# The second pass's x in the first pass's last stage: multiplication and low parts on GpSimd in place of VectorE

## The chip, the cores and the metric

One core of a Trainium2 chip runs the whole kernel. The metric is the device time of one execution in microseconds (us). TensorE (PE) does the matmuls, VectorE (DVE) and ScalarE (ACT) the work on elements, SyncE (SP) issues the DMAs, and GpSimd (POOL) has little to do. Each engine works through its own queue in order, and semaphores tie the queues together.

## The reference

An attention with capped scores, then two dense blocks with 768 inputs and 2048 inner columns:

```python
scores = cap * np.tanh((q @ k.T / sqrt(64)) / cap)       # 4 batches, 12 heads, 448 rows, 64 wide
attn = exp(scores - max) / (sum + 1e-09)
x = (attn @ v)  ->  (1792, 768)
h = x @ w_in;  x = (h - np.tanh(h)) @ w_out               # block 1
h = x @ w_in2; out = (h / (1 + np.exp(-1.702 * h))) @ w_out2   # block 2
```

All of it is float32 and the two weight matrices of a block come in float64.

## The kernel before

The 1792 rows are worked in two passes of two batches each (`NB = 2`, 896 rows per pass). The attention of all four batches comes first. Of batches 0 and 1 (first pass) its outputs stay on the chip; those of batches 2 and 3 (second pass) go to DRAM as 12 tiles `xd`, 128x448 each, together with rows `wrow` of reciprocal softmax sums. A pass then runs `gemm_in` and the output product of block 1, then block 2, whose last stage, `gemm_rows_seven`, writes the result.

Every matmul operand is split in two fp32r parts, a high part (a rounded copy: `hi_act` on ACT, line 76) and a low part (value minus high part: `lo_dve` on DVE, line 88, or `lo_pool` on GpSimd, line 82). A product is three matmuls: high x high, high x low, low x high. In the traces `wh`/`wl` are the parts of weights, `rh`/`rl` those of the left operand of the last stage, `xh`/`xl` those of x. As line 88 is one helper for all low parts, its rows are told apart by tile.

`gemm_rows_seven` (lines 967 to 1057) forms its product from seven smaller ones, p = 0 to 6, named in `SEVEN_B`. Each has four chunks of weights. `ahead` (line 1001) prepares the weights two chunks ahead (`LEAD = 2`, three buffers `wh`/`wl`): a DMA into `whole` or `pair`, the cast wh on ACT, the subtraction wl on DVE. `left(SEVEN_B[p + 1], k)` makes the left operand of the *next* small product (rh on ACT, rl on DVE). The results of a small product leave PSUM through line 985, 988 (`pair<-ps_o`, one PSUM and one SBUF input) or `rows_out` (lines 1063, 1069), which stores to DRAM. From p = 2 on, the first pass also does one step per chunk for the second pass's x: line 1027 loads a tile of x and its row sums (`x_load`: x in one of two buffers `far`, w in one of two buffers `t`, three DMAs on SP), and line 1025 scales the tile that was loaded two steps earlier (`x_scale`): x times w, the high part into `xh`, the low part into `xl`. A buffer of x is free for the next load once its low part is made. There are 12 tiles; all 12 pairs `xh`, `xl` are read in the first microseconds of the second pass (`gemm_in`, line 787).

In the attention stage GpSimd multiplies nothing; it casts and subtracts: the low parts of the first pass's x (`xl<-xs`, 128x448) and of nine early weight chunks (`wl<-wr`, 128x768).

Only the instructions of the attention stage are pinned to the order of the program (`pin`). In the later stages a scheduler at build time, by its own model of durations, sets the order in each engine's queue; on the chip that order is fixed.

Of the kernel before, what the change touches and what calls it, by code (L numbers as in the profile page):

```python
# [15 lines left out]
ALU = mybir.AluOpType  # L16
# [21 lines left out]
def attention_moe_moe(ctx, tc, q, k, v, cap, w_in1, w_out1, w_in2, w_out2, out):  # L38
    nc = tc.nc
    B, H, S, D = q.shape  # L40
# [31 lines left out]
    def pin(ins):  # L72
        return tc.keep_in_program_order(ins) if pinned[0] else ins

    def hi_act(dst, src):
        pin(nc.scalar.copy(out=dst, in_=src))  # L76
# [4 lines left out]
    def lo_pool(dst, src, hi):  # L81
        pin(nc.gpsimd.tensor_tensor(out=dst, in0=src, in1=hi.bitcast(F32), op=ALU.subtract))
# [4 lines left out]
    def lo_dve(dst, src, hi):  # L87
        pin(nc.vector.tensor_tensor(out=dst, in0=src, in1=hi.bitcast(F32), op=ALU.subtract))  # L88
# [12 lines left out]
    xh = [big.tile([P, NT], F32R, name=f"xh{i}") for i in range(KM)]  # L101
    xl = [big.tile([P, NT], F32R, name=f"xl{i}") for i in range(KM)]
# [432 lines left out]
    def x_split(s, i, x):  # L535
        a = slice(s * S, (s + 1) * S)
        hi_act(xh[i][:, a], x)
        lo_dve(xl[i][:, a], x, xh[i][:, a])
# [428 lines left out]
    def gemm_rows_seven(b0):  # L967
# [29 lines left out]
        for p, name in enumerate(SEVEN_B):  # L997
            ps = three()
            for j in range(KQ):
                i, (wh, wl) = w_next()  # L1000
                ahead(i)
                for kk in range(2):
                    k = 2 * j + kk
                    h, l = ring[k]
                    for n in range(3):
                        t = slice(n * P, (n + 1) * P)
                        for m, (x, w) in enumerate(((h, wh), (h, wl), (l, wh))):
                            nc.tensor.matmul(  # L1008
                                ps[n], x[:, t], w[:, kk, :],
                                start=(k == 0 and m == 0), stop=(k == KH - 1 and m == 2),  # L1010
                            )
                    if name == "11":
                        rest_products(k, k, 0, wh[:, kk, :], wl[:, kk, :], True, False)
                    elif name == "21":
                        rest_products(k, KH + k, 0, wh[:, kk, :], wl[:, kk, :], False, True)
                    elif name == "22":
                        rest_products(k, KH + k, 1, wh[:, kk, :], wl[:, kk, :], True, False)
                    if p < 6:
                        left(SEVEN_B[p + 1], k)
                if p == 0 and j == 0:  # L1020
                    run_late()
                if p < 2:
                    continue
                if len(loaded) > 1 or loaded and not todo:
                    x_scale(*loaded.pop(0))
                if todo:
                    loaded.append((*todo[0], *x_load(b0 + NB, *todo.pop(0))))
# [57 lines left out]
        return x, w  # L1085

    def x_scale(s, i, x, w):
        nc.vector.tensor_tensor(out=x, in0=x, in1=w, op=ALU.mult)
        x_split(s, i, x)

    def moe(b0):
        if b0 + NB == B:
# [76 lines left out]
```

## Time and profile before

| | |
|---|---|
| median of 3 runs | 1096.5 us (1094.42 to 1097.2) |
| profiled execution | 1100.42 us, of which the span of the trace is 1098.6 us |
| PE / DVE / ACT / POOL busy | 98% / 85% / 61% / 5% of the span |
| granted TensorE clock | 0.998 of full speed |

A row of the timeline gives start (us), duration (us), engine, line and operation, out<-in, and in brackets how long the engine idled before it and what ended that (`[1.17 <-DVE wl L88]`: 1.17 us, until the wl of line 88 on DVE was done). Consecutive instructions of an engine overlap in the records: the start of the next one tells when the engine was free, and an end is later than that. Matmuls are pipelined, so it is the distance between their starts that counts. Spans on POOL are rough.

### The profile page before, as it was taken

The numbers are of one execution on the slowest core, as the hardware profiler recorded it, in microseconds if no ns is written. First come the engines' busy times: TensorE is split into PE (matmuls) and PEld (weight loads), VectorE is DVE, ScalarE is ACT, GpSimd is POOL, SyncE is SP. The second block draws the span as 40 slices with busy tenths as digits, with TensorE's granted clock in tenths as the row PEclk, the third lists the DMA queues.
The fourth block names the chain that finished last, engine by engine and source line by source line (L and its number), as shares of the span: only waits on it lengthen the run. The fifth ranks groups of instructions, "written<-read, shape, count | busy, mean of one in ns | idle before, by whom it ended". The sixth has DMA issues, their size and how long they took to land.

```text
span 1098.6 us, 16113 instructions
## 1 busy us (share of the span) xinstructions
PE 1082.0 (98%) x5579; PEld 886.7 (81%) x5579; DVE 931.2 (85%) x1467; ACT 668.7 (61%) x1022; POOL 59.1 (5%) x56
## 2 busy tenths in 40 slices
PE   9999998999999999999999999999999999999998
PEld 3333333688899889889999998889999989999998
DVE  4788999799997787888796885899999898889774
ACT  6898888799893434444255554767655554455453
POOL 0013443200000000000000000000000000000000
PEclk9999999999999999999999999999999999999999
DMA  6766685455538899898735778888555243333344
GB/s 147 203 190 195 189 244 186 153 205 170 178 116 283 312 314 337 286 306 287 261 94 171 220 224 279 303 270 306 176 195 176 87 132 113 101 115 101 122 142 141
DMA packets 156466, 220.58 MB, mean 201 GB/s; under 512 B 58672, under 2 KB 108640, under 8 KB 156384
## 3 DMA queue, kind: packets, MB, share of 16 engines
q1 hardware_dynamic: 155088, 218.94, 62.4%
q8 instruction: 44, 0.72, 0.3%
q10 hardware_dynamic: 1296, 0.61, 0.2%
q14 instruction: 38, 0.31, 0.1%
HBM read 160.83 MB, written 58.68 MB: 200 GB/s over the span
## 4 chain that ended last, share of the span: by engine, by line
PE 71%; DVE 11%; DMA 7%; ACT 6%; issue 4%; SPq 1%; DVEq 0%; ACTq 0%
PE ps_h L787 21%; PE ps_o L1008 12%; PE ps_y L850 10%; PE ps_h L934 9%; PE ps_pv L497 7%; PE ps_sc L456 5%; DMA wd<-in_moe_w_out_dram 4%; PE ps_o L993 3%; DVE wr L185 1%; DVE wd L175 1%; DVE g_q L696 1%; DVE wl L88 1%; DVE g_t L694 1%; ACT wr L168 1%; PE ps_qk L435 1%
## 5 line engine op out<-in xcount | busy, mean ns | idle before, releaser
L787 PE MATMUL ps_h<-xl,wh 128*128 128x384 f32 (+1 forms) x576 | 210.6, 366 | 1.2 <-DVE xl L88 1.2
L787 PE MATMUL ps_h<-xh,wh 128*128 128x384 f32 (+1 forms) x576 | 209.5, 364 | 0.7 <-DMA wh<-kept 0.7
L76 ACT CAST rh<-gr 128x384 fp32r<-128x384 f32 (+1 forms) x141 | 73.8, 528 | 95.9 <-PE ps_o L1008 47.7
L787 PE MATMUL ps_h<-xh,wl 128*128 128x384 f32 (+1 forms) x576 | 131.1, 362 | 0.0
L787 PEld LDWEIGHTS ps_h<-xl,wh 128*128 128x128 f32 x576 | 108.1, 188 | 14.3 <-DVE xl L88 2.1
L787 PEld LDWEIGHTS ps_h<-xh,wh 128*128 128x128 f32 x576 | 108.1, 188 | 13.9 <-DMA wh<-kept 1.1
L1008 PE MATMUL ps_o<-wl,rh 128*128 128x384 f32 x336 | 112.6, 335 | 3.1 <-DVE wl L88 3.1
L76 ACT CAST wh<-whole 128x768 fp32r<-128x768 f32 (+1 forms) x105 | 84.8, 809 | 50.1 <-PE ps_h L934 37.1
L787 PEld LDWEIGHTS ps_h<-xh,wl 128*128 128x128 f32 x576 | 104.6, 188 | 12.6 <-issue 1.4
L1008 PE MATMUL ps_o<-wh,rh 128*128 128x384 f32 x336 | 112.3, 334 | 0.0
L1008 PE MATMUL ps_o<-wh,rl 128*128 128x384 f32 x336 | 112.2, 334 | 0.0
L88 DVE TENSOR_TENSOR wl<-whole,wh 128x768 fp32r<-128x768 f32 (+1 forms) x105 | 96.6, 923 | 7.9 <-ACT wh L76 6.7
L168 ACT ACTIVATE wr<-wd 128x768 f32<-128x768 f32 x64 | 57.9, 906 | 74.0 <-DMA wd<-in_moe_w_out_dram 37.8
L88 DVE TENSOR_TENSOR rl<-gr,rh 128x384 fp32r<-128x384 f32 (+1 forms) x141 | 79.9, 575 | 15.1 <-ACT rh L76 14.2
L475 ACT ACTIVATE t<-ps_sc,tsc 128x896 f32<-128x896 f32 x72 | 69.9, 1006 | 26.7 <-PE ps_sc L456 26.7
L175 DVE TENSOR_SCALAR wd<-wd 128x768 uint16<-128x768 uint16 x57 | 59.7, 1047 | 24.5 <-ACT wr L168 24.3
L477 ACT ACTIVATE t<-t,cpos 128x896 f32<-128x896 f32 x72 | 72.3, 1042 | 0.4
L812 PE MATMUL ps_y<-gh,wh 128*128 128x512 f32 (+1 forms) x192 | 70.0, 365 | 1.2 <-DVE xl L88 1.2
L812 PE MATMUL ps_y<-gl,wh 128*128 128x512 f32 (+1 forms) x192 | 69.9, 364 | 0.0
L456 PE MATMUL ps_sc<-qk 64*128 64x448 f32 x288 | 68.1, 571 | 0.8 <-ACT qk L76 0.6
L497 PE MATMUL ps_pv<-t,rv 128*64 128x448 f32 x288 | 64.4, 552 | 3.9 <-ACT t L475 3.4
L1008 PEld LDWEIGHTS ps_o<-wl,rh 128*128 128x128 f32 x336 | 63.1, 188 | 4.1 <-DVE wl L88 4.1
(145 smaller groups left out, 2311.3 us busy)
## 6 DMA issues: line engine op xcount, KB each, us to landing
wd<-in_moe_w_in_dram SPq DMA_DIRECT2D x64, 384.0 KB
wd<-in_moe_w_out_dram SPq DMA_DIRECT2D x32, 768.0 KB
single<-wr SPq DMA_DIRECT2D x48, 384.0 KB
whole<-single SPq DMA_DIRECT2D x43, 384.0 KB
pair<-single SPq DMA_DIRECT2D x40, 384.0 KB
s<-pair SPq DMA_DIRECT2D x32, 384.0 KB
whole<-s SPq DMA_DIRECT2D x32, 384.0 KB
wh<-kept SPq DMA_DIRECT2D x25, 384.0 KB
```

The costliest lines, as they stand in the source:

```text
L76: pin(nc.scalar.copy(out=dst, in_=src))
L88: pin(nc.vector.tensor_tensor(out=dst, in0=src, in1=hi.bitcast(F32), op=ALU.subtract))
L175: pin(nc.vector.tensor_scalar(out=half[:, :, 2], in0=half[:, :, 1], scalar1=F64_LOW, scalar2=None, op0=ALU.mult))
L456: pin(nc.tensor.matmul(ps[:, j, :S], qk[a, kc], qk[a, :S], start=True, stop=True))
L475: pin(nc.scalar.activation(out=t, in_=ps[:, :, :S], func=AF.Tanh, scale=tsc))
L477: ins = pin(nc.scalar.activation(out=tt[g, c], in_=tt[g, c], func=AF.Exp, scale=cpos))
L497: pin(nc.tensor.matmul(ps[a, :S], w, t[:, j], start=(c == 0), stop=(c == KC - 1)))
L787: pin(nc.tensor.matmul(ps, w[:, kk, :], x[kk][:, a], start=(m == 0), stop=(m == len(seq) - 1)))
L812: nc.tensor.matmul(bank[e][:, :a1 - a0], w[:, kk, c], x[2 * j + kk][:, a0:a1], start=(j == 0 and m == 0), stop=(j == KF // 2 - 1 and m == ...
L850: nc.tensor.matmul(ps[e], w[:, kk, c], x, start=(k == 0 and m == 0), stop=(k == KH - 1 and m == 2))
L934: nc.tensor.matmul(ps, w, x, start=(m == 0), stop=(m == len(seq) - 1))
L1008: nc.tensor.matmul(ps[n], x[:, t], w[:, kk, :], start=(k == 0 and m == 0), stop=(k == KH - 1 and m == 2),)
```

## The change

In `x_scale` the multiplication goes from DVE to GpSimd, the high part stays on ACT, and the low part goes from DVE (through `x_split`) to GpSimd. `x_scale` runs in the last stage of the first pass alone, 12 times.

```diff
     def x_scale(s, i, x, w):
-        nc.vector.tensor_tensor(out=x, in0=x, in1=w, op=ALU.mult)
-        x_split(s, i, x)
+        a = slice(s * S, (s + 1) * S)
+        nc.gpsimd.tensor_tensor(out=x, in0=x, in1=w, op=ALU.mult)
+        hi_act(xh[i][:, a], x)
+        lo_pool(xl[i][:, a], x, xh[i][:, a])
```

`x_split` was `hi_act` and `lo_dve` on the same tiles; `lo_pool` is the helper of line 82.

## Rows read from the trace of the kernel before

**Rows 1.** The page, busy us (share of the span) xinstructions: TensorE.
```profile
PE 1082.0 (98%) x5579; PEld 886.7 (81%) x5579; DVE 931.2 (85%) x1467; ACT 668.7 (61%) x1022; POOL 59.1 (5%) x56
```

**Rows 2.** Table of stretches: from:to us, length, then busy us (xinstructions) by engine.
```profile
core 0: us, PE busy (x) PEld busy (x) DVE busy (x) ACT busy (x) POOL busy (x), PEclk, DMA share, GB/s
598.00:650.00 52.00, 48.89 (x279) 47.93 (x278) 46.65 (x81) 32.21 (x56) 0.00 (x0) 1.00 0.71 217
650.00:664.00 14.00, 14.00 (x83) 14.00 (x82) 6.99 (x13) 3.28 (x5) 0.00 (x0) 1.00 0.68 205
```

**Rows 3.** Timeline of PE: the four waits between 598 and 666 us.
```profile
621.88 0.45 PE L1008 MATMUL ps_o<-wl,rh 128*128 128x384 f32 x1 [0.75 <-DVE wl L88]
...
626.48 0.44 PE L1008 MATMUL ps_o<-wl,rh 128*128 128x384 f32 x1 [1.19 <-DVE wl L88]
...
639.77 0.33 PE L1008 MATMUL ps_o<-wh,rl 128*128 128x384 f32 x1
639.94 0.34 PE L1008 MATMUL ps_o<-wh,rh 128*128 128x384 f32 x1
641.45 0.45 PE L1008 MATMUL ps_o<-wl,rh 128*128 128x384 f32 x1 [1.17 <-DVE wl L88]
...
665.18 0.50 PE L787 MATMUL ps_h<-xh,wh 128*128 128x512 f32 x1 [0.75 <-DMA wh<-kept]
```

**Rows 4.** Groups by line and shape, DVE, 598 to 650 us: busy us, mean ns | idle.
```profile
L88 DVE TENSOR_TENSOR rl<-gr,rh 128x384 fp32r<-128x384 f32 x23 | 12.3, 551 | 0.1
L88 DVE TENSOR_TENSOR wl<-whole,wh 128x768 fp32r<-128x768 f32 x11 | 10.4, 951 | 0.0
L1088 DVE TENSOR_TENSOR x<-x,w 128x448 f32<-128x448 f32 x12 | 7.4, 620 | 4.6 <-DMA x<-xd 2.8 <-DMA w<-wrow 1.8
L88 DVE TENSOR_TENSOR xl<-x,xh 128x448 fp32r<-128x448 f32 x12 | 7.4, 619 | 0.6 <-ACT xh L76 0.6
L988 DVE SCALAR_TENSOR_TENSOR pair<-ps_o,pair 128x384 f32<-128x384 f32 x12 | 6.0, 548 | 0.0
```

**Rows 5.** Waits, ACT, 598 to 665 us: us in total, times, longest us.
```profile
ACT xh L76 <- DVE x L1088: 9.3, 7, 2.5
```

**Rows 6.** Timeline of DVE around the three waits for wl.
```profile
617.46 0.63 DVE L1088 TENSOR_TENSOR x<-x,w 128x448 f32<-128x448 f32 x1 [1.79 <-DMA w<-wrow]
...
620.34 0.62 DVE L1088 TENSOR_TENSOR x<-x,w 128x448 f32<-128x448 f32 x1
620.88 0.95 DVE L88 TENSOR_TENSOR wl<-whole,wh 128x768 fp32r<-128x768 f32 x1
...
622.22 1.01 DVE L988 SCALAR_TENSOR_TENSOR pair<-ps_o,pair 128x384 f32<-128x384 f32 x2
...
625.48 0.95 DVE L88 TENSOR_TENSOR wl<-pair,wh 128x768 fp32r<-128x768 f32 x1
...
638.44 0.62 DVE L1088 TENSOR_TENSOR x<-x,w 128x448 f32<-128x448 f32 x1 [1.50 <-DMA x<-xd]
...
640.45 0.95 DVE L88 TENSOR_TENSOR wl<-whole,wh 128x768 fp32r<-128x768 f32 x1
```

**Rows 7.** Groups by line and shape, GpSimd, whole span.
```profile
L82 POOL TENSOR_TENSOR xl<-xs,xh 128x448 fp32r<-128x448 f32 x12 | 19.3, 1610 | 0.6
```

**Rows 8.** Timelines of GpSimd and DVE in the attention stage.
```profile
102.61 1.14 POOL L82 TENSOR_TENSOR xl<-xs,xh 128x448 fp32r<-128x448 f32 x1
103.71 2.66 POOL L82 TENSOR_TENSOR wl<-wr,wh 128x768 fp32r<-128x768 f32 x1
...
104.74 2.59 DVE L487 TENSOR_TENSOR ts<-ts,tl 64x896 f32<-64x896 f32 x1
...
121.88 1.09 DVE L487 TENSOR_TENSOR ts<-ts,tl 64x896 f32<-64x896 f32 x1
```

**Rows 9.** Timeline of ACT around two of the waits.
```profile
618.12 0.57 ACT L76 CAST xh<-x 128x448 fp32r<-128x448 f32 x1 [2.50 <-DVE x L1088]
...
619.01 0.83 ACT L76 CAST wh<-whole 128x768 fp32r<-128x768 f32 x1
...
636.23 0.83 ACT L76 CAST wh<-whole 128x768 fp32r<-128x768 f32 x1
```

**Rows 10.** Line 1088: duration ns min/median/max, first and last start us.
```profile
L1088 DVE TENSOR_TENSOR x<-x,w x12: 616/618/626, 598.4 to 646.0; 128x448 f32<-128x448 f32 x12
```

## The prediction

> **What bounds the kernel now.** I read the page first: TensorE (PE) is busy for 98% of the span [rows 1], so time can only be won where PE stands still, and each stand must be placed before it is priced. The change touches one stretch: the last stage of the first pass, about 590 to 664 us of the span, where the x of the second pass is loaded, multiplied and split beside the product. The table of stretches shows the core of it: between 598 and 650 us PE is busy for 48.89 of 52 us, VectorE (DVE) for 46.65, ScalarE (ACT) for 32.21, GpSimd (POOL) not at all; from 650 to 664 us PE is full again [rows 2]. The timeline of PE then gives the places. Matmuls of 384 columns start every 0.17 us (639.77 to 639.94). Three times the second matmul of a chunk, the first that reads a low part of the weights, waits for the subtraction on DVE that makes wl [rows 3]. From 639.94 to 641.45 us is 1.51 us where 0.17 is usual: 1.34 lost. The other two have idle times of 0.75 and 1.19 us instead of 1.17, so they lose 0.92 and 1.36. Each of the three matmuls also lasts about 0.11 us longer than the 0.34 of its neighbour. Together that is 1.03 + 1.47 + 1.45 = **3.95 us**, all that this stage loses. At its end comes one more wait of 0.75 us, for a DMA of stored weights (wh<-kept) [rows 3], which no edit touches.
>
> Why is wl late? DVE's 81 instructions of these 52 us include 12 multiplications (line 1088) and 12 subtractions xl, and DVE idles 4.6 us in front of the multiplications for the DMAs of x and w [rows 2, 4]. DVE works in order, so the weights' subtractions queue behind that. ACT stands 9.3 us, seven times, for the multiplication on DVE, and its casts of the weights (wh) queue behind that [rows 5].
>
> **The change part by part.**
>
> *Removed from DVE:* 24 instructions. They last 0.62 us, but successors start earlier: the multiplication at 620.34 is followed by the subtraction at 620.88, so a slot is 0.54 us [rows 4, 6]. 24 x 0.54 = 13.0 us, plus the 4.6 us of DMA waits. DVE keeps 46.65 - 13.0 = 33.7 us of work in 52.
>
> *Unchanged on ACT:* the 12 casts of xh. Their releaser becomes GpSimd.
>
> *Added on GpSimd:* 12 multiplications and 12 subtractions of 128x448. The subtraction is the form that GpSimd ran 12 times in the attention stage: 1.61 us mean [rows 7]; undisturbed it is 1.10 us, from its start at 102.61 to the next one's at 103.71 [rows 8]. No row shows the multiplication on GpSimd. From the slot of the subtraction (1.10, the same two inputs and shape) to its mean with disturbance (1.61) are my bounds, and I take 1.10 because the rest is counted as blocking below. 24 x 1.10 = 26.4 us on an engine that is empty here. By duration alone this is hidden.
>
> *GpSimd and DVE get in each other's way.* This is the cost that decides. In the attention stage a GpSimd subtraction began at 103.71 and lasted 2.66 us; the DVE addition at 104.74 beside it lasted 2.59 us, while the same line at 121.88, with GpSimd idle, took 1.09 [rows 8]: 1.5 us lost in one instruction, which ended about as long after the GpSimd one as it needs alone. The Trainium skill (SBUF — State Buffer, Who interferes with whom) says the same: a DVE instruction with two SBUF inputs and a GpSimd instruction that reads SBUF exclude each other for the whole instruction. By that rule, the trace agrees, offloading here pays DVE back less than its slots. In this stage nearly all that DVE keeps has two SBUF inputs: rl and wl. Only the 12 evictions (line 988) read PSUM and one SBUF input [rows 4]; I expect them to escape, which no row shows. If each GpSimd instruction blocks DVE in full, DVE needs 33.7 + 26.4 = 60.1 us, 8.1 more than the 52 it has; if they all fall into its gaps, nothing. Those are the bounds. The even guess is that DVE has something queued for about 60% of GpSimd's time (its load without x is 33.7 / 52 = 65%): 16 us of blocking, hence a load of 50 us out of 52. That is about where it stands today with its DMA waits (46.65 + 4.6 = 51.3). **So the engine whose relief is wanted is hardly relieved; only what it waits for changes.** The places then decide, one by one.
>
> *Stall at 641.45.* The wh for it was cast at 636.23 (ACT, 0.83 us) [rows 9]. The wl started only at 640.45, because DVE stood 1.50 us for the DMA of x, until 638.44, then multiplied, and later ran xl [rows 6]. Without these, 1.50 + 2 x 0.54 = 2.6 us, wl starts by 637.9 and ends before PE asks for it at 640.1: -1.45 us.
>
> *Stall at 626.48.* Its wl runs at 625.48 behind evictions that begin at 622.22. One multiplication (620.34) and one subtraction of x stand ahead of these: 2 x 0.54 = 1.1 us leave DVE's queue [rows 6]. -1.1 us.
>
> *Stall at 621.88.* ACT waited 2.50 us for the multiplication until 618.12, and only then cast wh (619.01) [rows 9]; the multiplication itself waited for the DMA of w until 617.46 [rows 6]. With GpSimd it takes 1.10 instead of 0.62 us and may first wait for a DVE instruction, so ACT goes on 0.5 to 1.4 us later. On the other side DVE drops one multiplication and one subtraction ahead of wl (1.1 us). Between -0.6 and +0.3: I take -0.15.
>
> *New blocking in front of wl.* A DVE instruction that meets GpSimd (busy 26.4 / 52 = half the time) waits half of 1.10: 0.28 us on average. With two others ahead of it in the queue that is 0.84 us for a wl. At two places (621.88 and 626.48) there is no slack against it: 2 x 0.84 = +1.7 us. Bounds 0 and +8.1, as above.
>
> *The chain of x.* The 12 multiplications start from 598.4 to 646.0 us [rows 10], one in 4.3 us, paced by two buffers: load, multiply, cast, subtract, and only then the next load on SP. GpSimd adds 2 x (1.10 - 0.62) = 1.0 us to a buffer's cycle, 0.5 per item, but the waits in DVE's queue go. The last split moves from 648 to anything between 645 and 655 us. The next pass needs it at 665.18 [rows 3]: covered, cost zero. If the cycle grew by more than 17 us in 11 items (1.5 us each), it would be the bound.
>
> **Sum:** -1.45 - 1.1 - 0.15 + 1.7 = -1.0 us. Against the profiled execution (1100.4 us, span 1098.6) that is 1099.4. The median of the three runs, 1096.5, lies 3.9 below that execution, so the forecast is **1095.5 us**.
>
> **The rivals.**
>
> *All three stalls go.* For it: DVE loses 17.6 us of work and waits at once. Against: rows 8. 1096.5 - 3.95 = 1092.5 us; nothing else in this stage is left to win.
>
> *The port becomes the bound, slower.* GpSimd and DVE exclude each other so often that DVE cannot keep up with wl. It decides from the point where more than 52 - 33.7 = 18.3 of GpSimd's 26.4 us block DVE, against my guess of 16. At the upper bound DVE runs 8.1 us over; the 3.95 us of today are in place of that: +4.1, **1100.6 us**. For it: 2.59 against 1.09 us in rows 8. Against: rl is made a product ahead, so part of the overrun can slide into 650 to 664 us, where DVE is busy for 6.99 of 14 us [rows 2].
>
> *ACT takes the waits over.* ACT in order stands for GpSimd instead of for DVE, 0.5 to 1.4 us longer per item: 12 x 0.5 = 6 us to 17 us, while it has 52 - 32.2 = 19.8 us of idle time, of which 9.3 are used up for x [rows 2, 5]. At the lower end the rest covers it and the three stalls stay as late casts: no change, 1096.5 us. At the upper end it adds to the slower case.
>
> *The change doesn't act:* the scheduler might order ACT and SP otherwise, since only instructions of the attention stage are pinned. That would spread each case by a microsecond, not change its sign.
>
> **How the numbers follow.** Forecast (two stalls shortened or gone, some blocking back; 1093.3 to 1097): 0.42. No change by ACT's waits or an even trade (1096 to 1099): 0.20. Port bound: 0.23. All stalls gone: 0.12. Chain of x late beyond 665 us: 0.03, above 1102. About 0.3%, 3.3 us, is what a measurement of this kernel can tell from no change. Faster by more than that (below 1093.2): 0.12 plus 0.02 of the forecast's edge = 0.14. Slower (above 1099.8): 0.21 of the port's case, 0.03 of x, 0.03 of ACT = 0.27. The rest, 0.59, is the same. The range takes in all stalls gone, 1092.0, and the port's case at its bound, 1101.0.
>
> **What would show it.** Right: POOL busy for 26 to 45 us between 598 and 655 us with spans of 1.1 to 2 us; DVE rows of rl and wl with a mean above today's 0.55 and 0.95 us; no wait of DVE for the DMAs of x and w; the stall near 640 us gone; one or two waits of PE for wl left near the ends of products. Wrong: DVE's means unchanged (no exclusion; then 1092.5), or PE waiting for wl more than three times and above 4 us in total (port or ACT; the waits of ACT for POOL then tell which), or PE waiting for xh or xl at the start of the second pass.

## The result

The changed kernel takes 1106.9 us in the median (4 runs, 1105.6 to 1109.4) against 1096.9 us for the kernel before on the same chip: ratio 1.0092, 95% interval 1.0071 to 1.0113. It is **slower by 10.0 us**, where a gain of 1.0 us was forecast, too small to tell from no change. The profiled execution took 1109.36 us, 1107.6 of it in the span.

The table of stretches, with the columns of [rows 2], shows the stage again:

```profile
598.00:650.00 52.00, 44.39 (x237) 42.01 (x236) 43.13 (x47) 26.28 (x47) 30.56 (x24) 0.97 0.67 201
```

PE is busy for 44.39 us where it was 48.89. DVE has 47 instructions left of 81, and is still busy for 43.13 us. GpSimd has its 24 instructions here.

The timeline of PE, the answer to [rows 3]: all waits of PE from 598 to 677 us that show an idle time.

```profile
614.01 0.44 PE L1008 MATMUL ps_o<-wh,rh 128*128 128x384 f32 x1 [1.68 <-ACT wh L76]
615.36 0.44 PE L1008 MATMUL ps_o<-wl,rh 128*128 128x384 f32 x1 [0.91 <-DVE wl L88]
...
626.04 0.44 PE L993 MATMUL ps_o<-wl,resth 128*128 128x384 f32 x1 [1.05 <-DVE wl L88]
629.74 0.44 PE L1008 MATMUL ps_o<-wl,rh 128*128 128x384 f32 x1 [2.32 <-DVE wl L88]
635.29 0.44 PE L1008 MATMUL ps_o<-wl,rh 128*128 128x384 f32 x1 [0.57 <-DVE wl L88]
...
647.34 0.45 PE L1008 MATMUL ps_o<-wl,rh 128*128 128x384 f32 x1 [1.07 <-DVE wl L88]
651.47 0.45 PE L1008 MATMUL ps_o<-wl,rh 128*128 128x384 f32 x1 [0.71 <-DVE wl L88]
...
676.22 0.50 PE L787 MATMUL ps_h<-xh,wh 128*128 128x512 f32 x1 [1.75 <-DMA wh<-kept]
```

Three waits of 3.1 us have become seven of 8.3 us. Counted as in the prediction, by the starts of the matmuls, the stage loses 12.1 us instead of 3.95, and the wait at its end 2.0 instead of 1.0: 9.1 us more. The two spans differ by 9.0 us, and that they agree so well is in part luck: with the change the stage begins 1.8 us later, and what comes behind it is 2.1 us shorter. After 677 us PE shows no wait of that size in either trace. The groups of DVE (598 to 665 us, columns of [rows 4]) say why wl is late:

```profile
L88 DVE TENSOR_TENSOR wl<-whole,wh 128x768 fp32r<-128x768 f32 x13 | 19.6, 1517 | 0.7 <-ACT wh L76 0.6
L88 DVE TENSOR_TENSOR rl<-gr,rh 128x384 fp32r<-128x384 f32 x24 | 19.1, 817 | 4.0 <-ACT rh L76 4.0
...
L988 DVE SCALAR_TENSOR_TENSOR pair<-ps_o,pair 128x384 f32<-128x384 f32 x12 | 6.0, 543 | 0.0
```

The mean of wl went from 951 to 1517 ns and that of rl from 551 to 817; the evictions of line 988, with one SBUF input, stayed (548, now 543) [rows 4]. This is what the Trainium skill (SBUF — State Buffer, Who interferes with whom) states: two SBUF inputs contend with a GpSimd instruction that reads, one does not; the trace agrees. The timelines of GpSimd and DVE show how they meet:

```profile
623.74 1.43 POOL L1089 TENSOR_TENSOR x<-x,w 128x448 f32<-128x448 f32 x1
627.73 1.14 POOL L1089 TENSOR_TENSOR x<-x,w 128x448 f32<-128x448 f32 x1 [0.73 <-DMA w<-wrow]
645.25 1.22 POOL L82 TENSOR_TENSOR xl<-x,xh 128x448 fp32r<-128x448 f32 x1 [0.68 <-ACT xh L76]
...
622.96 1.20 DVE L88 TENSOR_TENSOR rl<-gr,rh 128x384 fp32r<-128x384 f32 x1 [2.59 <-ACT rh L76]
624.09 1.90 DVE L88 TENSOR_TENSOR wl<-whole,wh 128x768 fp32r<-128x768 f32 x1
627.81 1.88 DVE L88 TENSOR_TENSOR wl<-whole,wh 128x768 fp32r<-128x768 f32 x1
645.38 1.90 DVE L88 TENSOR_TENSOR wl<-whole,wh 128x768 fp32r<-128x768 f32 x1
```

The multiplication issued at 623.74 lasts 1.43 us instead of 1.15, as it begins beside the last of rl. The wl of 624.09 comes next on DVE and lasts 1.90 us: it waits for the whole multiplication. At 627.73 and 645.25 GpSimd begins 0.1 us before wl, and wl again lasts 1.9. Between 600 and 650 us, 9 of the 13 wl last 1.73 to 1.91 us and four at most 0.96. **A wl pays nearly a whole GpSimd instruction or nothing.** Four of PE's seven waits, 5.15 of the 8.31 us, end right behind such a wl: those of 626.04, 629.74, 647.34 and 651.47 (the last behind this one):

```profile
649.58 1.83 DVE L88 TENSOR_TENSOR wl<-whole,wh 128x768 fp32r<-128x768 f32 x1
```

The other three do not. The one of 635.29 ends behind a wl of 0.94 us that stood behind six evictions. The first two, 2.59 us, begin at ACT. It stood in order for a multiplication on GpSimd, so its cast wh came late, and the wl after it, 0.95 us long, too:

```profile
612.25 0.56 ACT L76 CAST xh<-x 128x448 fp32r<-128x448 f32 x1 [2.29 <-POOL x L1089]
613.13 1.56 ACT L76 CAST wh<-whole 128x768 fp32r<-128x768 f32 x2
```

All of ACT's casts of x wait longer, the answer to [rows 5]:

```profile
ACT xh L76 <- POOL x L1089: 20.9, 12, 3.7
```

So there were three candidates. *Port*: GpSimd's reads shut DVE out. *ACT*: its casts stand in order behind the slower multiplication. *SP*: weight loads stand behind loads of x that wait for GpSimd (12.8 us of such waits, against 6.6 on DVE before). Of SP the trace of the change shows no effect on the weights: between 598 and 665 us no cast wh on ACT waits for a load, where they waited 2.1 us before.

### The profile page after: what moved, and what is told of

Same layout as the page of the kernel before. It is cut to its first block, busy times and chain, and to the rows that moved or that the text cites. A ratio compares the mean times of both kernels' runs of the same rounds, so it can differ in the third digit from the quotient of the medians.

```text
span 1107.6 us, 16134 instructions
## 1 busy us (share of the span) xinstructions
PE 1083.1 (98%) x5579; PEld 888.3 (80%) x5579; DVE 935.7 (84%) x1443; ACT 668.2 (60%) x1022; POOL 90.2 (8%) x80
## 4 chain that ended last, share of the span: by engine, by line
PE 76%; DVE 8%; DMA 7%; ACT 4%; issue 3%; SPq 1%; POOL 1%; ACTq 0%; DVEq 0%; POOLq 0%
PE ps_h L787 26%; PE ps_o L1008 13%; PE ps_y L850 9%; PE ps_h L934 9%; PE ps_pv L497 6%; PE ps_sc L456 5%; DMA wd<-in_moe_w_out_dram 4%; PE ps_o L993 3%; DVE wd L175 1%; PE ps_qk L435 1%; DVE wr L185 1%; PE ps_r L504 1%; ACT wr L168 1%; DMA wd<-in_moe_w_in_dram 1%; DVE wl L88 1%
## 5 line engine op out<-in xcount | busy, mean ns | idle before, releaser
L88 DVE TENSOR_TENSOR wl<-whole,wh 128x768 fp32r<-128x768 f32 (+1 forms) x105 | 103.9, 992 | 8.8 <-ACT wh L76 7.1
L88 DVE TENSOR_TENSOR rl<-gr,rh 128x384 fp32r<-128x384 f32 (+1 forms) x141 | 86.1, 619 | 20.2 <-ACT rh L76 19.2
```

## The experiments

Ratios are against runs of the kernel before on the same chip; "loss" is the time that PE loses in the stage plus the wait at its end, in the profiled execution, by the starts of the matmuls. One profiled execution can lie off the median: that of "multiplication only" is the fastest of its ten.

| kernel | GpSimd instructions that read | ratio (95%) | wl (whole) / rl (gr), mean ns | loss, us |
|---|---|---|---|---|
| before | 0 | 1 | 951 / 551 | 3.9 + 1.0 |
| the change | 24 | 1.0092 (1.0071 to 1.0113) | 1517 / 817 | 12.1 + 2.0 |
| multiplication only | 12 | 1.0037 (1.0015 to 1.0059) | 1199 / 669 | 6.2 + 0.8 |
| low part only | 12 | 1.0034 (1.0014 to 1.0055) | 1097 / 753 | 4.6 + 1.9 |
| added multiplications, result unused | 24 | 1.0161 (1.0130 to 1.0191) | 1322 / 810 | 19.9 + 1.0 |
| the change, four buffers | 24 | 1.0072 (1.0046 to 1.0099) | 1176 / 1039 | 9.7 + 2.3 |
| all of x on GpSimd | 36 | 1.0078 (1.0052 to 1.0104) | 1258 / 924 | 10.6 + 2.2 |
| all of x on GpSimd, four buffers | 36 | 1.0073 (1.0043 to 1.0103) | 1441 / 1060 | 10.1 + 1.4 |
| added writes | 0 (120 memsets) | 1.0008 (0.9989 to 1.0027) | 951 / 550 | 3.4 + 1.1 |

**Half of the change, either half.** In the first run only the multiplication moves, in the second only the low part:

```diff
-        nc.vector.tensor_tensor(out=x, in0=x, in1=w, op=ALU.mult)
+        nc.gpsimd.tensor_tensor(out=x, in0=x, in1=w, op=ALU.mult)
         x_split(s, i, x)
```
```diff
+        a = slice(s * S, (s + 1) * S)
         nc.vector.tensor_tensor(out=x, in0=x, in1=w, op=ALU.mult)
-        x_split(s, i, x)
+        hi_act(xh[i][:, a], x)
+        lo_pool(xl[i][:, a], x, xh[i][:, a])
```

> Only the multiplication of x goes to GpSimd; the low part stays on VectorE. Three theories for the 10.0 us that the change costs. Port (GpSimd and VectorE instructions with two SBUF inputs exclude each other): 12 of 24 GpSimd instructions are left, so about half, +5 us against before, and the stretch of rl and wl falls from 16.9 to about 8 us. ACT (ScalarE's cast of x stands in order for the slower multiplication, 20.9 us instead of 9.3): the multiplication is the whole cause, +7 to +10 us, and the waits of ACT for POOL stay near 20 us. SP (loads of weights stand behind loads of x that wait for GpSimd's low part): +0 to +3 us, as the low part is quick again.

> Only the low part of x goes to GpSimd; the multiplication stays on VectorE. Port: half of the GpSimd instructions, +5 us against before, stretch of rl and wl about 8 us. ACT: its casts wait for VectorE as before, so -1 to +1 us. SP: a buffer of x is held by GpSimd's subtraction, which starts only after the cast: +4 to +8 us, with waits of SP's loads of x for POOL near 12 us.

Measured: +4.1 us (1.6 to 6.5 by the interval) and +3.7 us (1.5 to 6.0), so each half costs somewhat less than half, and Port's +5 us lies in both intervals. In the first, ACT's waits stayed at 18.7 us and yet 6 of the 10 us were gone, which ACT did not allow; in the second ACT waited 6.4 us, less than before, and a loss remained. SP is not excluded by this pair: its +0 to +3 and +4 to +8 us overlap the intervals, and in the second its loads of x waited 11.2 us for GpSimd, as it expected.

**The reads alone.** x stays on DVE; GpSimd does two multiplications per tile whose result nobody uses:

```diff
+        a = slice(s * S, (s + 1) * S)
         nc.vector.tensor_tensor(out=x, in0=x, in1=w, op=ALU.mult)
         x_split(s, i, x)
+        for _ in range(2):
+            nc.gpsimd.tensor_tensor(
+                out=s2[0], in0=xl[i][:, a].bitcast(F32), in1=xh[i][:, a].bitcast(F32), op=ALU.mult
+            )
```

> All of x stays on VectorE and ScalarE as before; GpSimd runs two extra multiplications of the same shape per tile on the finished parts, into a tile that nobody reads (24 in all, added work that no result needs). Port: VectorE keeps its 24 instructions and is stretched as well, so +8 to +15 us against before, rl and wl longer by 12 to 17 us in sum. ACT and SP: nobody waits for these instructions, so 0 to +1 us.

Measured: +17.7 us, above the expected span. No instruction waits for these 24. Groups of DVE and a wait of PE in this run (DVE's 24 instructions for x are in it as well):

```profile
L88 DVE TENSOR_TENSOR rl<-gr,rh 128x384 fp32r<-128x384 f32 x23 | 18.3, 810 | 0.1
L1089 DVE TENSOR_TENSOR x<-x,w 128x448 f32<-128x448 f32 x11 | 14.4, 1305 | 0.0
...
PE ps_o L1008 <- DVE wl L88: 11.1, 6, 3.4
```

**GpSimd busy without reading:**

```diff
         x_split(s, i, x)
+        for _ in range(10):
+            nc.gpsimd.memset(s2[0], 0.0)
```

> All of x on VectorE and ScalarE as before; GpSimd runs 120 added memsets of 128x448 (added work that no result needs) through the same stretch, which write the SBUF and read nothing. If the loss with 24 extra two-input instructions (+17.7 us) came of GpSimd's reads shutting VectorE out, this one costs 0 to +1 us and the means of rl and wl stay at 0.55 and 0.95 us. If any GpSimd work beside the stage costs (semaphores, SBUF traffic, another order of the queues), it costs +5 us or more.

```profile
L88 DVE TENSOR_TENSOR wl<-whole,wh 128x768 fp32r<-128x768 f32 x14 | 13.2, 951 | 0.5 <-DMA out_dram<-o 0.5
L88 DVE TENSOR_TENSOR rl<-gr,rh 128x384 fp32r<-128x384 f32 x24 | 12.9, 550 | 0.1
L1092 POOL MEMSET gs<- 128x448 f32 x120 | 56.8, 473 | 399.8 <-DVE rl L88 392.9
```

GpSimd was busy for 56.8 us, nearly twice as long as with the change (31.2), and DVE's means did not move: ratio 1.0008. It is the reading that costs. The same section of the Trainium skill has this too, a GpSimd instruction that only writes does not stand in the way of one with two SBUF inputs, and the trace agrees.

**ACT and SP taken away.** All of x on GpSimd, so that ACT never waits for it; the change with four buffers of x and w (the free tiles `s2`) and loads three steps ahead, so that SP never waits for GpSimd; then both together:

```diff
-        hi_act(xh[i][:, a], x)
+        hi_pool(xh[i][:, a], x)
```
```diff
-        x = temp_p("far").tile([P, TC], F32, tag="far", name="x")[:, :S]
-        w = g_p.tile([P, TC], F32, tag="t", name="w")[:, :S]
+        n = (s * KM + i) % 4
+        x, w = s2[n], s2[4 + n]
...
+                if 4 * p + j < 10:
+                    continue
-                if len(loaded) > 1 or loaded and not todo:
+                if len(loaded) > 2 or loaded and not todo:
```

> Multiplication, high part and low part of x all on GpSimd; ScalarE no longer touches x. Port: 36 GpSimd instructions instead of 24, of which the 12 casts are shorter (0.82 us): worse than the change, +11 to +14 us against before. ACT: its 20.9 us of waits vanish, so -2 to +2 us against before. SP: the chain of x per tile is about as long as with the change (1.10 + 0.82 + 1.10 without the hops to ScalarE), so +4 to +8 us remain.

> The change with four buffers of x and of w instead of two (tiles that are free in this stage), loads three steps ahead of use, and the tiles of x at chunks 10 to 24 instead of 10 to 21 of the stage. GpSimd runs the same 24 instructions. Port: the stretch of rl and wl stays near 17 us and +5 to +9 us remain. ACT and SP: the loads no longer wait for GpSimd and the multiplications no longer wait for DMAs, so waits of SP's loads of x go from 12.8 to under 2 us, ACT's from 20.9 to under 12, and if these were the cause, 0 to +3 us remain.

> Multiplication, high part and low part on GpSimd, with four buffers of x and w: ScalarE never waits for x and SP's loads never wait for GpSimd, 36 GpSimd instructions that read remain. Port: +5 to +9 us against before, rl and wl stretched by 17 us or more. ACT and SP as the cause: -2 to +1 us.

Measured: 1.0078 (+8.6 us), 1.0072 (1.0046 to 1.0099, +7.9 us) and 1.0073 (1.0043 to 1.0103, +8.0 us). Port had asked for more in the first (+11 to +14), ACT for much less in the first and third. The first takes away ACT's waits for x alone: SP's loads of x waited 22.2 us for GpSimd in it, and ACT's casts of weights 21.1 us for their loads, so its 8.6 us are a mixture, and SP's +4 to +8 fits them as well. The second left ACT's waits at 21.7 us, against the expectation, since a multiplication on GpSimd mostly starts right behind the low part of the tile before, and ACT stands for it; SP's waits for GpSimd fell to 1.7 us. The third has no wait of ACT for x and one of SP for GpSimd (2.0 us), and is the cleanest:

```profile
L88 DVE TENSOR_TENSOR rl<-gr,rh 128x384 fp32r<-128x384 f32 x24 | 24.8, 1060 | 0.3 <-ACT rh L76 0.3
L88 DVE TENSOR_TENSOR wl<-whole,wh 128x768 fp32r<-128x768 f32 x14 | 20.0, 1441 | 1.3 <-ACT wh L76 1.3
...
PE ps_o L1008 <- DVE wl L88: 6.0, 3, 2.5
```

Without ACT's waits for x, and with next to none of SP for GpSimd, the kernel still loses 8.0 us (4.7 to 11.3), and each of PE's three waits for wl is longer than any before. It is no exact share of the 10.0: GpSimd reads 36 times here instead of 24, and the 12 casts of x have left ACT. Whether ACT and SP account for the other 2 us is not settled; the intervals of 1.0073 and 1.0092 overlap. The two waits that began at ACT with the change (614.01 and 615.36) are gone here.

**The longer way per tile, without reads.** Memsets on GpSimd between the multiplication and ACT's cast; in the second run kept in order:

```diff
+        a = slice(s * S, (s + 1) * S)
         nc.vector.tensor_tensor(out=x, in0=x, in1=w, op=ALU.mult)
+        for _ in range(2):
+            tc.keep_in_program_order(nc.gpsimd.memset(w, 0.0))
+        tc.keep_in_program_order(nc.gpsimd.memset(xh[i][:, a].bitcast(F32), 0.0))
         x_split(s, i, x)
```

> All of x's arithmetic on VectorE and ScalarE as before, but between the multiplication and ScalarE's cast stand three GpSimd memsets of 128x448 (two over w once it is used up, one over the place in xh that the cast then overwrites; 0.47 us each by the run with memsets alone, so about 1.4 us and a hop to GpSimd more per tile). GpSimd reads nothing. This gives ScalarE, the buffers and SP's queue the change's longer way per tile without its reads. ACT and SP as the cause: +4 us or more against before, waits of ACT above 20 us. Port: -1 to +2 us, rl and wl at 0.55 and 0.95 us.

> The run with three memsets per tile again, now with the memsets kept in the program's order on GpSimd, so that the one over xh really stands behind the two over w and holds ScalarE's cast back (in the first attempt the memsets of xh had run long before the stage and held nothing back). All arithmetic of x stays on VectorE and ScalarE; GpSimd reads nothing; about 1.4 us and a hop more per tile between multiplication and cast, and the buffers of x and w are held that much longer. ACT and SP as the cause: ACT's waits for x above 15 us and +4 to +9 us against before. Port: -2 to +2 us against before, rl and wl at 0.55 and 0.95 us.

The first attempt missed its purpose: without the order the memsets of xh ran before the stage. It gave 0.9983 (0.9967 to 0.9998). The second gave 1.0002 (0.9985 to 1.0018), and the waits on ACT were not those of the change either:

```profile
L1092 POOL MEMSET xh<- 128x448 f32 x12 | 5.7, 474 | 0.0
...
ACT xh L76 <- POOL xh L1092: 4.9, 4, 1.9
```

The scheduler put the casts of x later in ACT's queue: against the kernel before, each of them stands behind more of ACT's other casts, where with the change most stand behind fewer. So 1.4 us more per tile cost nothing that can be measured when the order allows for them; what 20 us of ACT's waits cost by themselves was not tried.

**Where the 3.95 us of before come from.** x on DVE as before: first with three tiles per small product instead of four; then with four buffers and loads three steps ahead (the edit of the four buffers above); then with four buffers, loads two steps ahead and no tile of x at the first chunk of p = 3 and 4. The first edit, and the loop of the third:

```diff
-                if len(loaded) > 1 or loaded and not todo:
+                if j and (len(loaded) > 1 or loaded and not todo):
                     x_scale(*loaded.pop(0))
-                if todo:
+                if j and todo:
```
```diff
+                if 4 * p + j < 10 or j == 0 and p < 5:
+                    continue
                 if len(loaded) > 1 or loaded and not todo:
```

> The kernel before, all of x on VectorE and ScalarE, but three tiles of x per small product instead of four: none at a product's first chunk. VectorE's density falls by 1.1 us of 13.6, where the evictions come. If the three stalls before come of VectorE being full: -1 to -3 us. If they come of its waits for the DMAs of x and w: -1 to +1 us.

> The kernel before with four buffers of x and w and loads three steps ahead, as in the run with four buffers on GpSimd, multiplication and low part on VectorE. If the waits of VectorE and ScalarE for the DMAs of x and w (4.6 and 9.3 us) made the three stalls, they go and it is -2 to -4 us against before, faster than both kernels. If VectorE is full anyway, -1 to +1 us.

> A candidate: all of x on VectorE and ScalarE, four buffers of x and w, and no tile of x at the first chunk of small products 3 and 4. It joins the two runs that lost 2.8 and 2.9 us in this stage and its seam by their traces, against 5.0 us before. If both reliefs add: -2 to -4 us against before. If one wait for wl at a product's end and the seam stay: -1 to -2 us.

Measured: 0.9992 (0.9972 to 1.0011), 0.9987 (0.9962 to 1.0011) and 0.9984 (0.9971 to 0.9998, 12 runs, 1095.2 against 1096.8 us). In the third, PE's waits for wl are down to one:

```profile
598.00:650.00 52.00, 51.74 (x298) 51.42 (x298) 48.34 (x85) 34.64 (x59) 0.00 (x0) 1.00 0.74 230
...
PE ps_o L1008 <- DVE wl L88: 0.3, 1, 0.3
```

DVE does all its 24 instructions for x and PE is busy for 51.74 of 52 us. Its loss by the trace is 1.5 us in place of 5.0; of these 3.5 us the times show 1.7 (0.2 to 3.2), with an interval that just leaves 1 out. It is the only kernel of the study built to be faster than both that measured so, by a margin hardly above the noise: the run with misplaced memsets, which was not meant to be faster, came out alike, and its trace loses 3.4 us.

## Why the prediction was wrong

*What bounds the stage:* right. The three waits for wl, 3.95 us, were the stake, and the trace of the run with x spread over more buffers and chunks shows that they came of DVE's order and its waits for DMAs: they go, but for 0.3 us, without any work leaving DVE. The wait at the end of the stage, which no edit was to touch, went from 1.0 to 2.0 us; its cause was not looked for.

*GpSimd's instructions:* right. 1.10 us was taken; undisturbed ones show 1.14 to 1.16 as durations, and GpSimd was busy for 31.2 us (26 to 45 expected). The evictions escape. The last split ended at 650.6 us (645 to 655 expected), well ahead of the second pass. DVE's waits for the DMAs of x and w are gone.

*The amount of blocking:* right, with some luck, as the share of 60% was an even guess. It gave 16 us. From the groups: 13 wl x (1.517 - 0.951) + 24 rl x (0.817 - 0.551) = 13.7 us, and another 3.2 us on the 12 instructions of the two smaller groups, 16.9 in all.

*What the blocking costs PE:* **wrong, and this is the step that failed** ("New blocking in front of wl", +1.7 us). It had a DVE instruction meet GpSimd at a random moment, so that it waits half of 1.10 us half of the time, 0.28 us, and it counted two places without slack. Neither held. Where both engines have a queue the timelines show them taking turns, so a wl comes right behind the start of a GpSimd instruction and waits for nearly all of it: 9 of 13 wl lost 0.8 to 0.95 us each. And places that had slack lost it, in part to rl that were blocked in the same way just ahead (1.20 us instead of 0.55 before the wl of 624.09). The stage came to 12.1 us where 3.95 - 2.7 + 1.7 = 2.95 had been summed: 4.7 at the three old places, 6.1 at new ones (3.1 of these at the two waits that begin at ACT), and 1.4 by the clock (below).

*The port rival* named the mechanism and the sign with a chance of 0.23, and sized it too low, at 1100.6 us, for two reasons. Its condition was a sum over the stretch (18.3 of 26.4 us must block); 16.9 us did, DVE was idle for 52 - 43.1 = 8.9 us, and PE starved all the same, because wl is wanted at a given moment and an idle moment elsewhere does not pay for it. And it set today's 3.95 us off against the overrun.

*The single places:* PE runs the same 600 matmuls of this stage in the same order in both kernels, so each wait can be followed by its place in that order. The one of 621.88 stands at 629.74 and was to stay (-0.15): it grew from 1.03 to 2.66 us, behind a wl of 1.88. The one of 626.48 stands at 635.29 and was to shrink to 0.4: it went from 1.47 to 1.0. The one of 641.45 stands at 651.47 and was to go: it went from 1.45 to 1.0, behind a wl of 1.83. The relief is there at these two; at the last, what is left is about what its wl was stretched by (0.88). New ones stand at 614.01 with 615.36, 626.04, 641.81 (0.28 us) and 647.34.

*ACT's waits:* the size was right (9.3 to 20.9 us, 6 to 17 more expected). That they carry the loss was a rival; the run without them still lost 8.0 us. They have a part in it all the same: beside the two waits of PE at 614.01 and 615.36, DVE idled 9.8 us for casts rh of ACT between 598 and 665 us, where it had been 1.5 before. How much of the 10.0 us that is stays open.

## What to carry to other kernels

Work with two SBUF inputs that moves from DVE to GpSimd is not taken off DVE when what stays there has two SBUF inputs as well: a GpSimd instruction that reads returns as a wait of nearly its whole length when such a DVE instruction is queued, here 16.9 us of waits for 13.0 us of slots given up. Price such a move at the instruction that somebody waits for, with a full GpSimd instruction in front of it, and not by the load of the engines over a stretch. Where DVE is late because it stands in order for a DMA, move the load, not the work; here that took PE's waits for wl from 3.1 to 0.3 us, and the time down by 1.7 us, hardly above the noise.

## What the runs showed of the hardware

TensorE's clock fell within the stage. With the change, matmuls start 0.32 us apart instead of 0.17 from 631.3 to 634.2 us; the granted clock there (columns of [rows 2]):

```profile
631.00:634.30 3.30, 3.30 (x13) 3.23 (x11) 3.30 (x9) 0.96 (x3) 0.00 (x0) 0.52 0.85 251
```

0.52 is about the lower level, 1.2 of 2.4 GHz. Before it fell, PE had stood for 1.05 us before 626.04 and for 2.32 us before 629.74. It cost some ten matmuls up to 0.15 us each, 1.4 of the 12.1 us, which the prediction had no term for. In the run with all of x on GpSimd and four buffers it fell twice (0.50 from 627.1 to 630.4 and from 640.7 to 644.1 us), 3.1 of the 10.1 us. In the kernel before, whose longest wait here is 1.19 us, the granted clock is 1.00 in the same stretches [rows 2]. The length of the longest stand does not settle it in these runs: with the multiplication alone on GpSimd PE stood for 2.1 us at once and the granted clock stayed at 1.00 from 598 to 650 us, while with the memsets in order it fell to 0.50 at 642.4 us after a stand of 1.94 us.
